# The scalars of a state-space recurrence: square roots moved from ScalarE's tables to VectorE, small steps packed in pairs, and all copies of the first FFT stage on ScalarE

## The chip, the cores and the metric

The kernel runs on one core of one Trainium2 chip. The metric is device time in microseconds (us) from launch to end; a number for a kernel is the median of several executions. Some executions are recorded by the hardware profiler. Its page and its trace give times counted from the start of the recorded span.

A core has five engines that each work through their own instruction queue in order: TensorE (PE in the profile, its weight loads PEld), VectorE (DVE), ScalarE (ACT), GpSimd (POOL) and SyncE (SP, which here only issues DMA transfers). They meet through semaphores[...].

## The reference, cut to what matters

Two branches work on the same `x` of 2048 positions by 1024 channels and are mixed by a gate per position.

```python
X = rfft2(x, axes=(-2, -1)); X = X * (w_r + 1j * w_i)
a = irfft2(X, s=(S, D)).astype(bfloat16)               # branch A

Lam = Lambda_re + 1j * Lambda_im                       # branch B, 1024 complex states
dt = exp(log_dt); Lam_bar = exp(dt * Lam)
B_bar = ((Lam_bar - 1.0) / Lam)[:, None] * (B_re + 1j * B_im)
h_t = Lam_bar * h_(t-1) + B_bar @ x_t                  # 2048 steps
b = 2 * Re(C @ h_t) + x * Dskip

g = sigmoid((x * gate_w).sum(-1)); out = g * a + (1 - g) * b
```

The change concerns how a few numbers per state are made from `Lambda_re`, `Lambda_im` and `log_dt` before branch B can start: the decay `r = exp(dt*Re Lam)`, the turn per step `thp` (in parts of a full turn), and the length `rho` and the angle of the complex factor `(Lam_bar - 1)/Lam`. The angle goes into a phase offset `beta`. The length needs a square root, the angle an arctangent.

## The kernel before, in words

**Branch A** is a 2-D FFT done with matrix products. In its first stage, `fstage(jj)` for jj = 0 to 7, two of sixteen slices of `x` (`xts[jj]`, loaded by `load_x`, 512 KB each, eight loads) are folded on VectorE into sums and differences: four instructions, L447 to L450, which write the tile `eo`. GpSimd mends the edge column with four tiny instructions, L452 to L455, in the order of the program. After every second slice, TensorE multiplies two `eo` tiles with the matrix `FW_sb` (L472 and L473), 8 products for each of four tiles `ps_f` in PSUM, and each `ps_f` is copied into the store `FX` (the same memory as `big`) by two copies of 128x512, L476 and L477. There are 16 such `ps_f` tiles and 32 copies; three `ps_f` can be alive at once. The names `eo` rotate over two buffers for even and two for odd jj, so `eo` of jj can be written only when TensorE has read `eo` of jj-4.

The second stage works in 16 groups: `fd(g)` (L488, copied out by L500), `bf_w(g)` (L511 to L520 into `ps_xe` and `ps_xo`, copied by L515 and L521, then multiplied with the filter by L525 to L528), and `bi(g)` (L546 to L549, copied by L550). The first `fd` reads all of `FX`.

**Branch B**: `ssm_pe` makes `B x` with TensorE (`psu`, L388) from the transposed `x` (`xT`) and the transposed B (`BT`); ScalarE scales it with `rho` or `nrho` (= -rho) on its way out (L390). `ssm_dve` turns by the phase tables `tab`, runs the scan with `r_sb` (L408) and turns back. The tables come from `tables(q)` (L357 to L368), which needs `thp` and `beta`.

**The scalars** sit at L278 to L344: small instructions on tiles of 128x8 numbers. ScalarE takes part with Exp (L279, L282), Sin (L304, L305), Sqrt (L323, L335), and a further Sin and Arctan (L339, L341).

**Loading**: SyncE issues the loads in the order of the program. The first transposed load, `load_BT(0)` (two of L211) with `load_xT(0)` behind it (two of L216), and all the B and filter loads behind those, do not start before the eight slices of `x` have landed: a copy of one column on GpSimd, L678 in the loop over `fstage`, writes into `BT` from the last slice and so holds them back. It stands in GpSimd's queue behind the edge columns of jj = 4 and ahead of those of jj = 5:

```python
for jj in range(8):
    for _ in fstage(jj):
        pass
    if jj == 4:
        nc.gpsimd.tensor_copy(out=BT[:, 0, 0, 0, 0:1], in_=xts[7][:, 0, 0:1])
        load_BT(0)
        load_xT(0)
```

**What sets the order**: in this part of the kernel GpSimd and SyncE keep the order in which the program is written. TensorE, VectorE and ScalarE do not: a scheduler of the framework orders their instructions by its own estimates when the program is built, so a change in one place can reorder them elsewhere. In the built program before, one product of `psu` stands in TensorE's queue ahead of ten of the sixteen first `fd` products.

Of the kernel before, what the change touches and what calls it, by code (L numbers as in the profile page):

```python
# [10 lines left out]
ACT = mybir.ActivationFunctionType  # L11
ALU = mybir.AluOpType
FP32 = mybir.dt.float32
BF16 = mybir.dt.bfloat16
I32 = mybir.dt.int32
# [7 lines left out]
P = 128  # L23
TC = 512
NCH = S // TC
MAGIC = 12582912.0
INV2PI = float(1.0 / (2.0 * np.pi))
TWO_PI_LO = 2.0 * float(np.nextafter(np.float32(np.pi), np.float32(0.0)))
# [108 lines left out]
def kernel(  # L137
# [17 lines left out]
    nc = tc.nc  # L155
    x = A_x[0]
# [23 lines left out]
    rp = ctx.enter_context(tc.tile_pool(name="rp", bufs=2))  # L180
# [77 lines left out]
    sp = cpool  # L258

    scr = rp.tile([P, 32, 8], FP32, name="scr", tag="su")  # L260
    scr_n = [0]

    def v8(name):
        if name in ("r_sb", "thp", "beta", "rho", "nrho"):
            return sp.tile([P, 8], FP32, name=name)
        scr_n[0] += 1
        return scr[:, scr_n[0] - 1, :]
# [7 lines left out]
    lre, lim, ldt = vec[:, 0, :], vec[:, 1, :], vec[:, 2, :]  # L275
    chpi = sp.tile([P, 1], FP32, name="chpi")
    nc.vector.memset(chpi, HALF_PI)
    dt = v8("dt")  # L278
    nc.scalar.activation(out=dt, in_=ldt, func=ACT.Exp)  # L279
    are = v8("are"); nc.vector.tensor_mul(out=are, in0=dt, in1=lre)  # L280
    r_sb = v8("r_sb")
    nc.scalar.activation(out=r_sb, in_=are, func=ACT.Exp)  # L282
    thp = v8("thp")
    nc.vector.scalar_tensor_tensor(out=thp, in0=lim, scalar=INV2PI, in1=dt, op0=ALU.mult, op1=ALU.mult)

    def frac(xx, n, nm, pool=sp, tag=None):
        kk = pool.tile([P, n], FP32, name=nm + "_k", **({"tag": tag} if tag else {}))
        nc.vector.tensor_scalar(out=kk, in0=xx, scalar1=MAGIC, scalar2=-MAGIC, op0=ALU.add, op1=ALU.add)
        nc.vector.tensor_sub(out=xx, in0=xx, in1=kk)
        nc.vector.tensor_scalar(out=kk.bitcast(I32), in0=xx.bitcast(I32), scalar1=0x7FFFFFFF, scalar2=None,  # L290
                                op0=ALU.bitwise_and)
        return xx, kk

    ang = sp.tile([P, 16], FP32, name="ang")
    nc.vector.tensor_copy(out=ang[:, 0:8], in_=thp)
    nc.vector.tensor_scalar_mul(out=ang[:, 8:16], in0=thp, scalar1=float(TC))
    rr, ra = frac(ang, 16, "ang")
    snc = sp.tile([P, 2, 16], FP32, name="snc")

    den = v8("den"); nc.vector.tensor_mul(out=den, in0=lre, in1=lre)  # L300
    den2 = v8("den2"); nc.vector.tensor_mul(out=den2, in0=lim, in1=lim)
    nc.vector.tensor_add(out=den, in0=den, in1=den2)
    inv = v8("inv"); nc.vector.reciprocal(out=inv, in_=den)
    nc.scalar.activation(out=snc[:, 0, :], in_=rr, func=ACT.Sin, scale=TWO_PI_LO)  # L304
    nc.scalar.activation(out=snc[:, 1, :], in_=ra, func=ACT.Sin, scale=-TWO_PI_LO, bias=chpi)  # L305
    sth, cth, sTC, cTC = snc[:, 0, 0:8], snc[:, 1, 0:8], snc[:, 0, 8:16], snc[:, 1, 8:16]
    sg = sp.tile([P, 8, 2], FP32, name="sg")
    nc.vector.tensor_scalar_mul(out=sg[:, :, 1], in0=sTC, scalar1=-1.0)
    nc.vector.tensor_copy(out=sg[:, :, 0], in_=sTC)
    lbi = v8("lbi"); nc.vector.tensor_mul(out=lbi, in0=r_sb, in1=sth)  # L310
    nr = v8("nr"); nc.vector.tensor_mul(out=nr, in0=r_sb, in1=cth)
    nc.vector.tensor_scalar_add(out=nr, in0=nr, scalar1=-1.0)
    t_a = v8("t_a"); nc.vector.tensor_mul(out=t_a, in0=nr, in1=lre)
    t_b = v8("t_b"); nc.vector.tensor_mul(out=t_b, in0=lbi, in1=lim)
    cr = v8("cr"); nc.vector.tensor_add(out=cr, in0=t_a, in1=t_b)
    t_c = v8("t_c"); nc.vector.tensor_mul(out=t_c, in0=lbi, in1=lre)
    t_d = v8("t_d"); nc.vector.tensor_mul(out=t_d, in0=nr, in1=lim)
    ci = v8("ci"); nc.vector.tensor_sub(out=ci, in0=t_c, in1=t_d)
    m2 = v8("m2"); nc.vector.tensor_mul(out=m2, in0=cr, in1=cr)
    m3 = v8("m3"); nc.vector.tensor_mul(out=m3, in0=ci, in1=ci)  # L320
    nc.vector.tensor_add(out=m2, in0=m2, in1=m3)
    mag = v8("mag")
    nc.scalar.activation(out=mag, in_=m2, func=ACT.Sqrt)  # L323
    rho = v8("rho")
    nc.vector.scalar_tensor_tensor(out=rho, in0=mag, scalar=2.0, in1=inv, op0=ALU.mult, op1=ALU.mult)
    nrho = v8("nrho")
    nc.vector.tensor_scalar_mul(out=nrho, in0=rho, scalar1=-1.0)
    hd = v8("hd"); nc.vector.tensor_add(out=hd, in0=mag, in1=cr)
    nc.vector.tensor_scalar_max(out=hd, in0=hd, scalar1=1e-30)
    nc.vector.reciprocal(out=hd, in_=hd)  # L330
    ht = v8("ht"); nc.vector.tensor_mul(out=ht, in0=ci, in1=hd)
    nc.vector.tensor_scalar(out=ht, in0=ht, scalar1=-1e15, scalar2=1e15, op0=ALU.max, op1=ALU.min)
    hq = v8("hq"); nc.vector.tensor_mul(out=hq, in0=ht, in1=ht)
    nc.vector.tensor_scalar_add(out=hq, in0=hq, scalar1=1.0)
    nc.scalar.activation(out=hq, in_=hq, func=ACT.Sqrt)  # L335
    nc.vector.tensor_scalar_add(out=hq, in0=hq, scalar1=1.0)
    nc.vector.reciprocal(out=hq, in_=hq)
    nc.vector.tensor_mul(out=ht, in0=ht, in1=hq)
    nc.scalar.activation(out=hd, in_=ht, func=ACT.Sin)  # L339
    fq = v8("fq")  # L340
    nc.scalar.activation(out=fq, in_=ht, func=ACT.Arctan)  # L341
    beta = v8("beta")
    nc.vector.tensor_scalar_mul(out=beta, in0=thp, scalar1=-255.5)
    nc.vector.scalar_tensor_tensor(out=beta, in0=fq, scalar=-2.0 * INV2PI, in1=beta, op0=ALU.mult, op1=ALU.add)  # L344

    tau_i = rp.tile([P, TC], I32, name="tau_i", tag="su")
    nc.gpsimd.iota(tau_i, pattern=[[1, TC]], base=0, channel_multiplier=0)
# [3 lines left out]
    def tables(q):  # L351
        xa = rp.tile([P, 2 * TC], FP32, name="xa", tag="cu")
        for jj in range(2):
            jb = 2 * q + jj
            xj = xa[:, TC * jj:TC * (jj + 1)]
            if q < 2:
                nc.vector.tensor_scalar(out=xj, in0=tau_f, scalar1=thp[:, jb:jb + 1], scalar2=beta[:, jb:jb + 1],  # L357
                                        op0=ALU.mult, op1=ALU.add)
            else:
                nc.scalar.activation(out=xj, in_=tau_f, func=ACT.Identity, scale=thp[:, jb:jb + 1],  # L360
                                     bias=beta[:, jb:jb + 1])
        rr, ra = frac(xa, 2 * TC, "xa", rp, "su")
        tq = tab[:, 2 * q:2 * q + 2]
        rr = rr.rearrange("p (a t) -> p a t", a=2)
        ra = ra.rearrange("p (a t) -> p a t", a=2)
        nc.scalar.activation(out=tq[:, :, 0, :], in_=ra, func=ACT.Sin, scale=-TWO_PI_LO, bias=chpi)
        nc.scalar.activation(out=tq[:, :, 1, :], in_=rr, func=ACT.Sin, scale=-TWO_PI_LO)
        nc.vector.tensor_scalar_mul(out=tq[:, :, 2, :], in0=tq[:, :, 1, :], scalar1=-1.0)  # L368
# [74 lines left out]
    def fstage(jj):  # L443
# [10 lines left out]
        nc.gpsimd.tensor_sub(out=eo[:, :, 1, 1, 0:1], in0=om, in1=eo[:, :, 1, 0, 0:1])  # L454
        nc.gpsimd.tensor_add(out=eo[:, :, 1, 0, 0:1], in0=om, in1=eo[:, :, 1, 0, 0:1])  # L455
        eos[jj] = eo
        if jj % 2 == 0:
            return
        j0 = 2 * jj - 2
        for eo_i in range(2):  # L460
            for b in range(2):
                ps = psF.tile([P, 4, 2, P], FP32, name="ps_f", tag="ps")
                bs = slice(P * b, P * (b + 1))
                for jl in range(4):
                    jt = jj - 1 + jl // 2
                    v = eos[jt][:, jl % 2, eo_i]
                    if jt in () and eo_i == 0:
                        los = [xts[jt][:, jl % 2, 512 * h + P * b:512 * h + P * (b + 1)] for h in range(2)]
                    else:
                        los = [v[:, 0, bs]]  # L470
                    for i, lo in enumerate(los):
                        nc.tensor.matmul(ps[:, jl], lhsT=lo, rhs=FW_sb[:, 0:2 * P], start=(i == 0), stop=False)  # L472
                    nc.tensor.matmul(ps[:, jl], lhsT=v[:, 1, bs], rhs=FW_sb[:, P * (1 + eo_i):P * (3 + eo_i)],  # L473
                                     start=False, stop=True)
                q = 4 * eo_i + 2 * b
                nc.scalar.copy(out=FX[:, q, :, j0:j0 + 4], in_=ps[:, :, 0, :].rearrange("p j c -> p c j"))  # L476
                (nc.vector.tensor_copy if (eo_i, b) in ((1,0),(1,1)) else nc.scalar.copy)(  # L477
                    out=FX[:, q + 1, :, j0:j0 + 4], in_=ps[:, :, 1, :].rearrange("p j c -> p c j"))
                yield 1.0

# [365 lines left out]
```

## Time and profile before

| what | value |
|---|---|
| median of 4 runs | 352.89 us (352.27 to 353.61) |
| the profiled execution's own time | 352.43 us |
| its span in the profile | 350.6 us |
| TensorE busy | 326.1 us, 93% of the span |
| VectorE busy | 297.6 us, 85% |
| ScalarE busy | 188.2 us, 54% |
| GpSimd busy | 42.2 us, 12% |
| last of the eight slices of `x` landed | 17.67 us (issued 9.94, landing 7.73 later) |
| first `psu` product | 29.27 us |

The profiled time is 1.83 us longer than its span. Busy shares are averages over stages with different limits; the stages of interest here are the first 40 us. In the trace's answers a line gives start, duration, engine, source line and operation, the tiles written and read, and in square brackets how long the engine stood idle before and what ended that. `SPq` and `ACTq` are issues of DMA transfers, which don't count as busy.

### The profile page before, as it was taken

The numbers are of one execution on the slowest core, as the hardware profiler recorded it, in microseconds if no ns is written. First come the engines' busy times: TensorE is split into PE (matmuls) and PEld (weight loads), VectorE is DVE, ScalarE is ACT, GpSimd is POOL, SyncE is SP. The second block draws the span as 40 slices with busy tenths as digits, with TensorE's granted clock in tenths as the row PEclk, the third lists the DMA queues.
The fourth block names the chain that finished last, engine by engine and source line by source line (L and its number), as shares of the span: only waits on it lengthen the run. The fifth ranks groups of instructions, "written<-read, shape, count | busy, mean of one in ns | idle before, by whom it ended". The sixth has DMA issues, their size and how long they took to land.

```text
span 350.6 us, 4890 instructions
## 1 busy us (share of the span) xinstructions
PE 326.1 (93%) x1804; PEld 173.6 (50%) x1804; DVE 297.6 (85%) x419; ACT 188.2 (54%) x255; POOL 42.2 (12%) x89
## 2 busy tenths in 40 slices
PE   2888999799979999999999999999989998999995
PEld 1675666466636566464444444444434443444442
DVE  3998859977999969898999999989798798988431
ACT  1997979679957877687253325241413404322240
POOL 4330422122110000000011000000000000000110
PEclk9999999989989999999999999999999999999999
DMA  7999999979796122113995054322413323444863
GB/s 270 349 140 213 221 230 212 185 157 198 179 225 111 63 98 81 62 60 125 226 235 166 12 167 119 92 90 62 150 41 110 92 60 109 103 134 135 265 194 112
DMA packets 68168, 51.30 MB, mean 146 GB/s; under 512 B 52656, under 2 KB 55728, under 8 KB 68144
## 3 DMA queue, kind: packets, MB, share of 16 engines
q1 hardware_dynamic: 64144, 38.75, 44.1%
q0 software_dynamic: 3648, 12.07, 14.1%
q8 instruction: 14, 0.23, 0.3%
q10 hardware_dynamic: 352, 0.17, 0.2%
q14 instruction: 10, 0.08, 0.1%
HBM read 21.61 MB, written 8.39 MB: 86 GB/s over the span
## 4 chain that ended last, share of the span: by engine, by line
PE 59%; DVE 20%; DMA 7%; ACT 7%; issue 4%; SPq 2%; POOL 0%; DVEq 0%; ACTq 0%; POOLq 0%
PE psy L782 26%; PE psu L388 20%; DVE su L408 7%; DMA xc<-in_A_x_dram 3%; PE ps_id L557 3%; PE ps_d L488 2%; ACT X L500 2%; DVE cu L403 2%; DVE cu L433 2%; DMA CT<-in_A_x_dram 2%; DMA xT<-in_A_x_dram 1%; PE ps_q L546 1%; DMA xt<-in_A_x_dram 1%; ACT u L390 1%; DVE t L526 1%
## 5 line engine op out<-in xcount | busy, mean ns | idle before, releaser
L388 PE MATMUL psu<-xT,BT 128*128 128x512 bf16 x512 | 121.2, 381 | 5.5 <-ACT u L390 4.2
L388 PEld LDWEIGHTS <-BT 128*128 128x128 bf16 x512 | 50.0, 98 | 61.7 <-issue 7.7
L408 DVE TENSOR_TENSOR_SCAN su<-r_sb,carry,cu 128x512 bf16<-128x512 f32 x48 | 57.7, 1265 | 0.4
L390 ACT ACTIVATE u<-psu,rho 128x512 bf16<-128x512 f32 x32 | 22.1, 690 | 65.2 <-PE psu L388 41.6
L767 POOL DMA_DIRECT2D xf<-gac x16 | 14.0, 873 | 216.7 <-ACT xf L766 216.7
L782 PEld LDWEIGHTS <-h 128*128 128x128 bf16 x256 | 25.1, 98 | 30.2
L390 ACT ACTIVATE u<-psu,nrho 128x512 bf16<-128x512 f32 x32 | 22.1, 691 | 29.3 <-PE psu L388 29.3
L764 ACT ACTIVATE gac<-gac,gf 128x1024 bf16<-128x1024 bf16 x16 | 18.3, 1141 | 28.1 <-DMA gac<-ya_scratch 28.1
L782 PE MATMUL psy<-CT,h 128*128 128x512 bf16 x128 | 28.9, 379 | 0.0
L782 PE MATMUL psy<-big,h 128*128 128x512 bf16 x128 | 28.9, 379 | 0.0
L760 DVE TENSOR_TENSOR xc<-xc,dsk_bc 128x1024 bf16<-128x1024 bf16 x16 | 11.0, 686 | 18.9 <-DMA xc<-in_A_x_dram 18.9
L789 DVE SCALAR_TENSOR_TENSOR o<-psy,om_f,xf 128x1024 bf16<-128x1024 f32 (+1 forms) x17 | 20.6, 1215 | 6.3 <-PE psy L782 6.3
L399 DVE TENSOR_TENSOR cu<-u,tab 128x2048 bf16<-128x2048 bf16 x16 | 19.5, 1220 | 5.4 <-ACT u L390 5.3
L550 ACT CAST big<-ps_q 128x1024 bf16<-128x1024 f32 x16 | 16.4, 1028 | 10.7 <-PE ps_q L549 10.5
L546 PE MATMUL ps_q<-MM,Y 128*128 128x256 bf16 x64 | 15.7, 280 | 4.7 <-DVE Y L527 4.6
L782 PEld LDWEIGHTS <-big 128*128 128x128 bf16 x128 | 12.5, 98 | 15.1
L782 PEld LDWEIGHTS <-xT 128*128 128x128 bf16 x128 | 12.5, 98 | 15.1
L403 DVE TENSOR_TENSOR cu<-cu,su 128x2048 bf16<-128x2048 bf16 x16 | 19.6, 1227 | 0.3
L433 DVE TENSOR_TENSOR cu<-su,tab 128x2048 bf16<-128x2048 bf16 x16 | 19.5, 1220 | 0.1
L488 PE MATMUL ps_d<-G_sb,big 128*128 128x256 bf16 (+3 forms) x128 | 19.6, 294 | 0.0
L435 DVE TENSOR_TENSOR u<-su,tab 128x2048 bf16<-128x2048 bf16 x16 | 19.5, 1218 | 0.0
L401 DVE TENSOR_TENSOR su<-u,tab 128x2048 bf16<-128x2048 bf16 x16 | 19.5, 1218 | 0.0
(168 smaller groups left out, 560.8 us busy)
## 6 DMA issues: line engine op xcount, KB each, us to landing
xf<-gac POOLq DMA_DIRECT2D x16, 512.0 KB, 4.1
ya_scratch<-ya SPq DMA_DIRECT2D x16, 256.0 KB, 2.0
xc<-in_A_x_dram SPq DMA_DIRECT2D x16, 256.0 KB, 3.2
gac<-ya_scratch SPq DMA_DIRECT2D x16, 256.0 KB, 3.3
out_dram<-o SPq DMA_DIRECT2D x15, 256.0 KB, 2.0
MM<-c_MM SPq DMA_DIRECT2D x16, 192.0 KB, 4.2
xt<-in_A_x_dram SPq DMA_DIRECT2D x4, 512.0 KB, 4.4
CT<-in_A_x_dram SPq DMA_DIRECT2D x4, 512.0 KB, 7.7
```

What stands on the lines that cost most here:

```text
L388: nc.tensor.matmul(psu, lhsT=BT[:, jb, ri, dblk, :], rhs=xT[:, dblk, TC * c:TC * (c + 1)], start=(dblk == 0), stop=(dblk == 7))
L390: nc.scalar.activation(out=u[:, jj, ri, :], in_=psu, func=ACT.Copy, scale=(nrho if ri else rho)[:, jb:jb + 1])
L399: nc.vector.tensor_mul(out=cu, in0=u, in1=tq[:, :, 0:1, :].to_broadcast(full))
L401: nc.vector.tensor_mul(out=su, in0=u[:, :, ::-1, :], in1=tq[:, :, 1:3, :])
L403: nc.vector.tensor_add(out=cu, in0=cu, in1=su)
L408: nc.vector.tensor_tensor_scan(out=su[:, jj, ri, :], data0=r_sb[:, jb:jb + 1].to_broadcast([P, TC]), data1=cu[:, jj, ri, :], initial=(0.0 ...
L433: nc.vector.tensor_mul(out=cu, in0=su, in1=tq[:, :, 0:1, ::-1].to_broadcast(full))
L435: nc.vector.tensor_mul(out=u, in0=su[:, :, ::-1, :], in1=tq[:, :, 1:3, ::-1])
L488: nc.tensor.matmul(ps[:, lo:lo + w], lhsT=FX[:, q, 8 * g:8 * g + 8, :], rhs=G_sb[:, o:o + w], start=start, stop=stop, skip_group_check=True)
L546: nc.tensor.matmul(dst, lhsT=Yr[:, e:e + 255:2], rhs=ri_, start=True, stop=False, **kw)
L782: nc.tensor.matmul(psy[:, ds], lhsT=hs[c, jb // 2][:, jb % 2, ri, P * tq:P * (tq + 1)], rhs=CT[dh][:, jb, ri, :], start=(i == 0), stop=(i ...
L789: nc.vector.scalar_tensor_tensor(out=o[:, ds], in0=psy[:, ds], scalar=om_f[:, tb:tb + 1], in1=xfs[tb][:, ds], op0=ALU.mult, op1=ALU.add)
```

## The change

The edits are these.

1. Both square roots become an inverse square root computed on VectorE (`rsqrt`): a first guess from the bits of the number and two Newton steps, seven dependent small instructions. The half-angle form of the arctangent is rewritten to need one such root, no square root of `1 + t*t`, and the Sin at L339 goes.
2. Real and imaginary parts are packed in pairs of 16 numbers where both get the same operation (`nl`, `pr`, `c2`).
3. Six small instructions go to GpSimd: two for |Lam|^2, `nrho`, the first half of `beta`, and the two of `sg`.
4. The scalars are a generator, `scalars()`. Its first piece is emitted before the first stage, and one further piece at the end of the folding of each `fstage(jj)`, jj = 0 to 5. This sets where its GpSimd instructions stand in GpSimd's queue: |Lam|^2 behind the edge columns of jj = 0, `nrho` behind those of jj = 3, `beta` and `sg` behind those of jj = 5.
5. All 32 copies of the first stage are made by ScalarE; before, eight of them (L477 for the second half of each set of four) were VectorE's.

```diff
-    dt = v8("dt")
-    nc.scalar.activation(out=dt, in_=ldt, func=ACT.Exp)
...
-    mag = v8("mag")
-    nc.scalar.activation(out=mag, in_=m2, func=ACT.Sqrt)
-    rho = v8("rho")
-    nc.vector.scalar_tensor_tensor(out=rho, in0=mag, scalar=2.0, in1=inv, op0=ALU.mult, op1=ALU.mult)
-    nrho = v8("nrho")
-    nc.vector.tensor_scalar_mul(out=nrho, in0=rho, scalar1=-1.0)
...
-    nc.scalar.activation(out=hq, in_=hq, func=ACT.Sqrt)
...
-    nc.scalar.activation(out=hd, in_=ht, func=ACT.Sin)
-    fq = v8("fq")
-    nc.scalar.activation(out=fq, in_=ht, func=ACT.Arctan)
...
+    def rsqrt(y, x, s):
+        nc.vector.tensor_scalar(out=y.bitcast(I32), in0=x.bitcast(I32), scalar1=-0.5, scalar2=float(0x5F3759DF),
+                                op0=ALU.mult, op1=ALU.add)
+        for _ in range(2):
+            nc.vector.tensor_mul(out=s, in0=y, in1=y)
+            nc.vector.scalar_tensor_tensor(out=s, in0=s, scalar=-0.5, in1=x, op0=ALU.mult, op1=ALU.mult)
+            nc.vector.scalar_tensor_tensor(out=y, in0=s, scalar=1.5, in1=y, op0=ALU.add, op1=ALU.mult)
+
+    def scalars():
+        dt, are = v8("dt"), v8("are")
+        nc.scalar.activation(out=dt, in_=ldt, func=ACT.Exp)
...
+        yield
+        dd, inv = v16(), v8("inv")
+        nc.gpsimd.tensor_mul(out=dd, in0=lam, in1=lam)
+        nc.gpsimd.tensor_add(out=dd[:, 0, :], in0=dd[:, 0, :], in1=dd[:, 1, :])
+        nc.vector.reciprocal(out=inv, in_=dd[:, 0, :])
+        yield
+        nl, pr, c2 = v16(), v16(), v16()
+        nc.vector.tensor_mul(out=nl, in0=snc[:, ::-1, 0:8], in1=r_sb.unsqueeze(1).to_broadcast([P, 2, 8]))
...
+        yield
+        m2, rs, mag, s = v8("m2"), v8("rs"), v8("mag"), v8("s")
+        nc.vector.tensor_mul(out=pr, in0=c2, in1=c2)
+        nc.vector.scalar_tensor_tensor(out=m2, in0=pr[:, 0, :], scalar=1e-30, in1=pr[:, 1, :], op0=ALU.add, op1=ALU.add)
+        rsqrt(rs, m2, s)
+        nc.vector.tensor_mul(out=mag, in0=m2, in1=rs)
+        yield
+        nc.vector.scalar_tensor_tensor(out=rho, in0=mag, scalar=2.0, in1=inv, op0=ALU.mult, op1=ALU.mult)
+        nc.gpsimd.tensor_scalar_mul(out=nrho, in0=rho, scalar1=-1.0)
...
+        yield
+        rsqrt(rs, m2, s)
...
+        yield
...
+        nc.scalar.activation(out=fq, in_=hd, func=ACT.Arctan)
+        nc.gpsimd.tensor_scalar_mul(out=beta, in0=thp, scalar1=-255.5)
+        nc.vector.scalar_tensor_tensor(out=beta, in0=fq, scalar=-2.0 * INV2PI, in1=beta, op0=ALU.mult, op1=ALU.add)
+        nc.gpsimd.tensor_scalar_mul(out=sg[:, :, 1], in0=sTC, scalar1=-1.0)
+        nc.gpsimd.tensor_copy(out=sg[:, :, 0], in_=sTC)
+        yield
+
+    chain = scalars()
+    for _ in range(1):
+        next(chain, None)
...
         eos[jj] = eo
+        for _ in range(1):
+            next(chain, None)
         if jj % 2 == 0:
             return
...
-                (nc.vector.tensor_copy if (eo_i, b) in ((1,0),(1,1)) else nc.scalar.copy)(
+                (nc.vector.tensor_copy if (jj, eo_i, b) in () else nc.scalar.copy)(
                     out=FX[:, q + 1, :, j0:j0 + 4], in_=ps[:, :, 1, :].rearrange("p j c -> p c j"))
```

The built program after the change has the same order on SyncE. On TensorE, VectorE and ScalarE the order differs in the first stage and in the first groups of the second, and is the same from there on. Three of the differences matter below: VectorE folds jj = 2 before it has finished jj = 1; `rho` stands on VectorE behind the first folding instruction of jj = 6; and TensorE has all sixteen of the first `fd` products ahead of `psu`, with seven `psu` products then in a row ahead of the first `ps_xe`.

More of the change, by code (lines that the diff above doesn't have):

```diff
@@ L277 @@
     nc.vector.memset(chpi, HALF_PI)
-    dt = v8("dt")
-    nc.scalar.activation(out=dt, in_=ldt, func=ACT.Exp)
[L280 to L287, printed above, removed]
+    r_sb, beta, rho, nrho = (v8(n) for n in ("r_sb", "beta", "rho", "nrho"))
@@ L288, in frac @@
+    ang = sp.tile([P, 16], FP32, name="ang")
+    angk = rp.tile([P, 2, 16], FP32, name="angk", tag="cu")
+    snc = sp.tile([P, 2, 16], FP32, name="snc")
+    thp = ang[:, 0:8]
+    sTC, cTC = snc[:, 0, 8:16], snc[:, 1, 8:16]
+    sg = sp.tile([P, 8, 2], FP32, name="sg")
+    lam = scr[:, 28:30, :]
+    def frac(xx, kk, ff):
         nc.vector.tensor_scalar(out=kk, in0=xx, scalar1=MAGIC, scalar2=-MAGIC, op0=ALU.add, op1=ALU.add)
-        nc.vector.tensor_sub(out=xx, in0=xx, in1=kk)
-        nc.vector.tensor_scalar(out=kk.bitcast(I32), in0=xx.bitcast(I32), scalar1=0x7FFFFFFF, scalar2=None,
+        nc.vector.tensor_sub(out=ff, in0=xx, in1=kk)
+        nc.vector.tensor_scalar(out=kk.bitcast(I32), in0=ff.bitcast(I32), scalar1=0x7FFFFFFF, scalar2=None,
@@ L291, in frac @@
                                 op0=ALU.bitwise_and)
[L292 to L321, printed above, removed]
-    mag = v8("mag")
-    nc.scalar.activation(out=mag, in_=m2, func=ACT.Sqrt)
-    rho = v8("rho")
-    nc.vector.scalar_tensor_tensor(out=rho, in0=mag, scalar=2.0, in1=inv, op0=ALU.mult, op1=ALU.mult)
-    nrho = v8("nrho")
-    nc.vector.tensor_scalar_mul(out=nrho, in0=rho, scalar1=-1.0)
@@ L328 @@
[L328 to L334, printed above, removed]
-    nc.scalar.activation(out=hq, in_=hq, func=ACT.Sqrt)
@@ L336, with v16 @@
-    nc.vector.tensor_scalar_add(out=hq, in0=hq, scalar1=1.0)
-    nc.vector.reciprocal(out=hq, in_=hq)
-    nc.vector.tensor_mul(out=ht, in0=ht, in1=hq)
-    nc.scalar.activation(out=hd, in_=ht, func=ACT.Sin)
-    fq = v8("fq")
-    nc.scalar.activation(out=fq, in_=ht, func=ACT.Arctan)
-    beta = v8("beta")
-    nc.vector.tensor_scalar_mul(out=beta, in0=thp, scalar1=-255.5)
-    nc.vector.scalar_tensor_tensor(out=beta, in0=fq, scalar=-2.0 * INV2PI, in1=beta, op0=ALU.mult, op1=ALU.add)
+    def v16():
+        scr_n[0] += 2
+        return scr[:, scr_n[0] - 2:scr_n[0], :]
@@ new lines, in rsqrt @@
+    def rsqrt(y, x, s):
[8 more added lines that the diff above has]
+        nc.scalar.activation(out=dt, in_=ldt, func=ACT.Exp)
+        nc.vector.scalar_tensor_tensor(out=thp, in0=lim, scalar=INV2PI, in1=dt, op0=ALU.mult, op1=ALU.mult)
+        nc.vector.tensor_scalar_mul(out=ang[:, 8:16], in0=thp, scalar1=float(TC))
+        frac(ang, angk[:, 0, :], angk[:, 1, :])
+        nc.scalar.activation(out=snc[:, 0, :], in_=angk[:, 1, :], func=ACT.Sin, scale=TWO_PI_LO)
+        nc.scalar.activation(out=snc[:, 1, :], in_=angk[:, 0, :], func=ACT.Sin, scale=-TWO_PI_LO, bias=chpi)
+        nc.vector.tensor_mul(out=are, in0=dt, in1=lre)
+        nc.scalar.activation(out=r_sb, in_=are, func=ACT.Exp)
+        yield
[6 more added lines that the diff above has]
+        nc.vector.tensor_mul(out=nl, in0=snc[:, ::-1, 0:8], in1=r_sb.unsqueeze(1).to_broadcast([P, 2, 8]))
+        nc.vector.tensor_scalar_add(out=nl[:, 0, :], in0=nl[:, 0, :], scalar1=-1.0)
+        nc.vector.tensor_mul(out=pr, in0=nl, in1=lam)
+        nc.vector.tensor_add(out=c2[:, 0, :], in0=pr[:, 0, :], in1=pr[:, 1, :])
+        nc.vector.tensor_mul(out=pr, in0=nl[:, ::-1, :], in1=lam)
+        nc.vector.tensor_sub(out=c2[:, 1, :], in0=pr[:, 0, :], in1=pr[:, 1, :])
+        yield
[7 more added lines that the diff above has]
+        nc.gpsimd.tensor_scalar_mul(out=nrho, in0=rho, scalar1=-1.0)
+        hd = v8("hd")
+        nc.vector.tensor_add(out=hd, in0=mag, in1=c2[:, 0, :])
+        nc.vector.tensor_scalar_max(out=hd, in0=hd, scalar1=1e-20)
+        nc.vector.tensor_mul(out=m2, in0=hd, in1=mag)
+        yield
+        rsqrt(rs, m2, s)
+        nc.vector.tensor_mul(out=m2, in0=m2, in1=rs)
+        nc.vector.scalar_tensor_tensor(out=hd, in0=m2, scalar=float(np.sqrt(2.0)), in1=hd, op0=ALU.mult, op1=ALU.add)
+        nc.vector.reciprocal(out=hd, in_=hd)
+        yield
+        nc.vector.tensor_mul(out=hd, in0=c2[:, 1, :], in1=hd)
+        nc.vector.tensor_scalar(out=hd, in0=hd, scalar1=-1.0, scalar2=1.0, op0=ALU.max, op1=ALU.min)
+        fq = v8("fq")
+        nc.scalar.activation(out=fq, in_=hd, func=ACT.Arctan)
[4 more added lines that the diff above has]
+        yield
@@ L361, in tables @@
                                      bias=beta[:, jb:jb + 1])
-        rr, ra = frac(xa, 2 * TC, "xa", rp, "su")
+        kk = rp.tile([P, 2 * TC], FP32, name="xa_k", tag="su")
+        frac(xa, kk, xa)
+        rr, ra = xa, kk
         tq = tab[:, 2 * q:2 * q + 2]
```

## The prediction

> **What bounds the kernel now.** I read the page's busy line first, then the chain that ended last around the first stage, then each engine's timeline there.
>
> ```profile
> PE 326.1 (93%) x1804; PEld 173.6 (50%) x1804; DVE 297.6 (85%) x419; ACT 188.2 (54%) x255; POOL 42.2 (12%) x89
> ```
>
> TensorE bounds the whole, so a change in the first 30 us counts by how it moves the point from which TensorE is kept busy. Beyond the first groups of the second stage the built orders agree on all engines, so I carry a shift there to the end one to one. The chain of waits, in order of time:
>
> ```profile
> 19.51 1.30 SPq L211
> 20.85 3.09 SPq L216
> 23.99 5.14 DMA xT<-in_A_x_dram
> 29.13 0.14 issue
> 29.27 0.38 PE psu L388
> ...
> 30.22 1.93 ACT X L500 x2
> 32.15 0.64 ACT X L515
> ```
>
> Not VectorE or ScalarE but the transposed load `xT` releases TensorE at 29.27, and what follows is ScalarE's work without a gap. What starts that load is in the timelines of GpSimd, SyncE and TensorE:
>
> ```profile
> 14.71 0.20 POOL L455 TENSOR_TENSOR eo<-om,eo 128x2 bf16<-128x2 f32 x1
> 17.72 0.37 POOL L678 COPY BT<-CT 128x1 bf16<-128x1 bf16 x1 [2.81 <-DMA CT<-in_A_x_dram]
> 18.05 0.20 POOL L452 TENSOR_TENSOR eo<-CT 128x2 bf16<-128x2 bf16 x1
> 18.12 1.34 SPq L211 DMA_TRANSPOSE BT<-in_B_B_re_dram  x1
> 29.27 0.38 PE L388 MATMUL psu<-xT,BT 128*128 128x512 bf16 x1 [1.25 <-DMA xT<-in_A_x_dram]
> ```
>
> GpSimd was idle 2.81 us when the last slice of `x` landed (17.67). From L678's start, 17.72, to `psu` is 11.55 us of issues and landing. VectorE and ScalarE, for prices:
>
> ```profile
> 12.50 0.17 DVE L312 TENSOR_SCALAR scr<-scr 128x8 f32<-128x8 f32 x1
> 12.70 0.17 DVE L313 TENSOR_TENSOR scr<-scr 128x8 f32<-128x8 f32 x1
> 12.79 0.16 DVE L317 TENSOR_TENSOR scr<-scr 128x8 f32<-128x8 f32 x1
> 13.62 1.28 ACT L323 ACT_TABLE_LOAD   x1
> 14.20 0.68 DVE L477 CAST big<-ps_f 128x512 bf16<-128x512 f32 x1
> 14.80 0.42 DVE L449 TENSOR_TENSOR eo<-CT 128x510 bf16<-128x510 bf16 x1
> 15.13 0.42 DVE L450 TENSOR_TENSOR eo<-CT 128x510 bf16<-128x510 bf16 x1
> ```
>
> A small instruction that needs the one before it follows after 0.20 (12.50 to 12.70); one that doesn't, after 0.08. A folding instruction takes 0.34 start to start, VectorE's copy of `ps_f` 0.60. ScalarE's copies start 0.48 apart (20.82, 21.30, 21.78 in its timeline).
>
> [...] The trace has the 1.28 (10.46, 13.62, 19.17)[...]: the next instruction follows at once. I use 1.3. [...] here a dependent one costs 0.12 more[...]. [...] four edge instructions take 0.97 from 18.05 to 19.02, and 1.47 beside the last folding, from 21.11 to 22.58. [...] Here products fall from 0.42 to 0.28 at 12.11, 3.6 us after TensorE resumed at 8.51.
>
> **The change, part by part.**
>
> ScalarE loses two table loads (sqrt, then back to sine; 2 x 1.3) and three activations (3 x 0.2), and gains eight copies (8 x 0.48 = 3.8): +0.6 us. VectorE loses eight copies (8 x 0.60 = 4.8 us) and keeps as many small instructions (39 before, 40 after; packing pays for the Newton steps). Taken alone this would end VectorE's part earlier. But TensorE does not wait for VectorE at 29.27, so I credit none of it.
>
> The start. VectorE folds jj = 2 ahead of jj = 1 and must wait for that slice, which lands at 8.02. The third folding of jj = 1, which the first tiles need, has four foldings and four small instructions ahead of it from there: 8.05 + 4 x 0.34 + 4 x 0.08 = 9.73 for its start rather than 8.07. Six products at the slow clock's 0.21 then move the first ScalarE copy from 9.36 to about 11.3. TensorE idles meanwhile and reaches the full clock near 12.8. From 14.3 ScalarE is steadily fed, at 0.96 per tile.
>
> When `rho` is ready. Ahead of it on VectorE from 8.05: 21 foldings at 0.337 = 7.1, 17 small ones at 0.08 = 1.4, four dependent Newton links at 0.20 = 0.8, so 17.3. In between, folding jj = 4 overwrites a tile that the fourth `ps_f` still reads; TensorE comes to it near 13.8 instead of 12.9, +0.9. So `rho` starts at about 18.2 and ends at 18.35.
>
> GpSimd's queue. `nrho` waits for that, and behind it stand the four edge instructions of jj = 4 and then L678. So 18.4, plus 0.2 to 0.4 for `nrho`, plus 0.97 to 1.47: L678 starts at 19.65 to 20.25, and I take 19.9. That is 2.2 us later than 17.72. The idle 2.81 us is used up, because `rho` is made after 17.67.
>
> What is late next. All four transposes are 2.2 us late: `xT` lands at 31.3, `psu` starts at 31.45. The edge columns also hold the tiles of jj = 4 and 5, ScalarE starves about 1.5 us near 19.2, and `FX` is complete at about 14.3 + 13 x 0.96 + 1.5 + 0.4 (last landing and Arctan) = 28.7, against 28.46 before. The first `fd` products end near 29.4, so TensorE idles until 31.45.
>
> Reordering gives some back. Before, `ps_xe` started at 31.29, 2.02 after `psu`, with ten `fd` products in between. Now only seven `psu` products stand between, 7 x 0.216 = 1.5: `ps_xe` at 32.96, +1.67. ScalarE's L515 (32.04 before) follows its last product: 32.96 + 0.33 + 0.27 + 0.04 = 33.6, +1.56. From there to L550 (38.28 before) ScalarE has seven instructions of the same kinds in either order, with no gap: the shift stays. Half a microsecond of cover is thin elsewhere: the filter matrices `MM` come through SyncE's queue, also 2 us late, and one of them landed at 51.71 for a product at 52.07. That allows 0.36, so the shift may grow to about 1.7. Gaps of the chain after that are releases between engines that all shift.
>
> Sum: span 350.6 + 1.65 = 352.25. The profiled execution took 1.83 more than its span: 354.1. The median of the runs was 0.46 above the profiled 352.43, so I predict 354.5 us for the median.
>
> Unknown rows. GpSimd on 128x8 and 128x16 tiles: not in the trace; between the 0.2 of its 128x2 rows and VectorE's 0.17 doubled, 0.35. Only `nrho` matters, and both ends are in the range of L678. A Newton step with integer bits on VectorE: like other 128x8 rows, 0.16 to 0.20. Bounds of L678: 18.7 if TensorE's cold start costs nothing, 20.8 if each row is at its dear end and the links cost 0.25. That is a shift from +0.4 to +2.6.
>
> **The rivals.**
>
> *Hidden, or a small gain.* If L678 starts by 18.2, the new order (1.5 between `psu` and `ps_xe` instead of 2.0) outweighs the delay. With no delay `ps_xe` starts at 29.27 + 1.51 = 30.8 and ScalarE comes to L515 at 31.4, a gain of 0.65 us and no more: 352.89 - 0.65 = 352.2 as a median. For it speaks the idle 2.81 us of GpSimd; against it, that 21 foldings alone need 7.1 us from 8.05. A delay of 1.0 would leave +0.4, 353.3: no change that can be told.
>
> *ScalarE becomes the bound.* With 32 copies and an Arctan in the midst that waits for the end of the chain on VectorE (near 22.7), `FX` would be late. For it: 16 tiles x 0.96 = 15.4 us, from 11.3. Against: the copies end at 28.7, and only from about 30.5 would they delay `ps_xe` more than `xT` does. If the chain is 2.5 us later than I think, this adds about 0.7: 355.2.
>
> *SyncE's queue lags on.* It issues almost without a gap from 18 to 52 us. If the full 2.2, or 2.8 with GpSimd slow, reaches `MM` in groups 5 and 6, the shift is 2.4: 355.3.
>
> *The clock.* Twice in the trace the granted clock is halved for 3.4 us after TensorE idled (70 to 74 and 101 to 104; 0.76 over 70 to 77). Another phase of the same waits can add or spare one of these, up to 1.7 us: 352.8 or 356.2.
>
> **How the numbers follow.** About 0.3% (1.06 us) is what a measurement of this kernel can tell from no change: 351.83 to 353.95. Forecast, a shift of 1.1 to 2.2: 0.45. ScalarE or SyncE beyond it: 0.18. Clock dearer: 0.05, cheaper 0.08. Hidden or a small rest: 0.17. Something that I don't see and that gains: 0.07. So slower 0.68 (forecast, the two beyond it, the dear clock), faster 0.12 (the unseen gain and a part of the cheap clock), same 0.20. For 8 in 10 the range goes from 352.0, the hidden case, to 356.4; the forecast's own is 353.9 to 355.0.
>
> **What would show it.** L678's row starts near 19.9, behind `nrho` and not behind a transfer. `psu`'s row waits for `xT` by 1.5 to 2.5 us, with `fd` products done before. ACT shows two table loads in the first 30 us and 32 copies 0.48 apart with a hole near 19. If L678 still starts at 17.7, or `psu` no longer waits for a transfer, the forecast is wrong at its root.

## The result and the profile after

The kernel after took 356.61 us in the median of 44 runs (352.16 to 360.95), the kernel before 353.47 us in 63 runs (350.04 to 358.5; the four known ones are among them). The ratio is 1.0049, with a 95% interval of 1.0029 to 1.0068: slower by half a per cent, 1.7 us on 353. Applied to the 352.89 us that were known, it is 354.6. Medians in this document are of all executions, while a ratio compares only those within 1.5% of the fastest of their kernel (26 of the 44 of after and, by the same rule, 53 of the 63 of before), so the two medians lie further apart, 3.1 us, than the ratio says. The profiled execution of after took 356.14 us and its span is 354.3 us.

All readings below give microseconds from the start of the span, in the columns that the prediction's lines have. First GpSimd's and SyncE's timelines of after, at the trigger of the transposed loads, and TensorE's at the first `psu`:

```profile
18.66 0.45 POOL L336 TENSOR_SCALAR nrho<-rho 128x8 f32<-128x8 f32 x1 [5.22 <-DVE scr L338]
...
20.38 0.19 POOL L697 COPY BT<-CT 128x1 bf16<-128x1 bf16 x1
20.60 1.33 SPq L211 DMA_TRANSPOSE BT<-in_B_B_re_dram  x1
30.62 1.67 PE L405 MATMUL psu<-xT,BT 128*128 128x512 bf16 x7 [1.00 <-DMA xT<-in_A_x_dram]
```

The trigger (L678 before, L697 now) no longer waits for a transfer. `nrho` waits 5.22 for VectorE, and nothing that stands behind it in GpSimd's queue starts before it: four edge instructions follow from 19.06 on, and then the trigger, at 20.38 instead of 17.72. But `psu` starts at 30.62, 10.24 after the trigger where before took 11.55, and TensorE waits for `xT` by 1.00 where it waited 1.25. Of the 1.31 less, 1.20 lie in the first transpose of `x`: from its issue to that of the second it took 3.14 before (20.85 to 23.99) and 1.94 after (23.95 to 25.89). The conversion L534 (L515 before) comes at 32.76 instead of 32.04 and L569 (L550 before) at 38.92 instead of 38.28. So at 39 us the whole delay is +0.6.

The time is lost five microseconds later. The waits of TensorE in the first 130 us of after (total, number, longest):

```profile
PE ps_xe L530 <- DMA MM<-c_MM: 3.4, 1, 3.4
...
PE psu L405 <- DMA xT<-in_A_x_dram: 1.0, 1, 1.0
```

The profile before has no wait on `MM` in that list. The chain that ended last, after:

```profile
23.95 1.89 SPq L216
25.89 2.19 SPq L216
...
36.58 2.26 SPq L211
38.89 2.45 SPq L211
41.44 5.20 DMA MM<-c_MM
46.69 0.28 PE ps_xe L530
```

It no longer runs through `xT` and ScalarE, as before, but through SyncE's row of issues to the load of one filter matrix, that of group 3. SyncE's timeline at this load, first before:

```profile
35.05 1.31 SPq L211 DMA_TRANSPOSE BT<-in_B_B_re_dram  x1
36.40 1.51 SPq L211 DMA_TRANSPOSE BT<-in_B_B_im_dram  x1
38.14 0.40 SPq L232 DMA_DIRECT2D MM<-c_MM  x1
```

and after:

```profile
36.58 2.26 SPq L211 DMA_TRANSPOSE BT<-in_B_B_re_dram  x1
38.89 2.45 SPq L211 DMA_TRANSPOSE BT<-in_B_B_im_dram  x1
41.44 0.54 SPq L232 DMA_DIRECT2D MM<-c_MM  x1
```

The two transposes ahead of the matrix took 2.82 to issue before and 4.71 after. TensorE's first product with this matrix, before and after:

```profile
42.52 0.27 PE L511 MATMUL ps_xe<-X,MM 128*128 128x256 bf16 x1
46.69 0.28 PE L530 MATMUL ps_xe<-X,MM 128*128 128x256 bf16 x1 [3.43 <-DMA MM<-c_MM]
```

The matrix landed at 41.81 before, 0.71 ahead of its product at 42.52. After, it landed at 46.64, for a product at 46.69. The 4.83 that it is later are 2.66 of later trigger, 0.64 more between trigger and issue (21.06 against 20.42), and 1.53 more from issue to landing (5.20 against 3.67).

From there the delay, taken as the same instruction of ScalarE in both traces, is +3.75 to 67 us, +2.44 from 73 to 244 us, 1.8 to 2.0 to 290 us and +3.7 at the end. The two large later steps are stretches of 3.41 us at half the clock of TensorE (granted clock 0.50 in all four, 1.00 just before). Each of the two traces has two of them there, one of them at different places: before from 70.1 and 100.9, after from 103.0 and 294.2.

### The profile page after: what moved, and what is told of

Read it like the earlier page. It is cut to its first block, busy times and chain, and to the rows that moved or that the text cites. A ratio compares the mean times of both kernels' runs of the same rounds, so it can differ in the third digit from the quotient of the medians.

```text
span 354.3 us, 4895 instructions
## 1 busy us (share of the span) xinstructions
PE 327.0 (92%) x1804; PEld 173.7 (49%) x1804; DVE 294.4 (83%) x412; ACT 188.7 (53%) x258; POOL 44.1 (12%) x95
## 4 chain that ended last, share of the span: by engine, by line
DVE 37%; PE 35%; DMA 9%; issue 6%; SPq 6%; ACT 5%; POOL 1%; DVEq 0%; ACTq 0%; POOLq 0%
PE psy L801 15%; DVE su L425 14%; PE psu L405 7%; DMA xc<-in_A_x_dram 4%; SPq L211 3%; DVE cu L420 3%; DVE cu L450 3%; PE ps_id L576 3%; DVE u L452 3%; DVE o L808 2%; DVE su L418 2%; DVE xc L779 2%; DVE cu L416 2%; DMA MM<-c_MM 1%; PE ps_d L507 1%
## 5 line engine op out<-in xcount | busy, mean ns | idle before, releaser
L569 ACT CAST big<-ps_q 128x1024 bf16<-128x1024 f32 x16 | 16.4, 1027 | 10.1 <-PE ps_q L568 9.8
L801 PEld LDWEIGHTS <-xT 128*128 128x128 bf16 x128 | 12.9, 101 | 16.2 <-issue 1.9
L507 PE MATMUL ps_d<-G_sb,big 128*128 128x256 bf16 (+3 forms) x128 | 18.7, 286 | 0.2 <-ACT big L496 0.2
```

Source lines behind the costliest of these rows:

```text
L507: nc.tensor.matmul(ps[:, lo:lo + w], lhsT=FX[:, q, 8 * g:8 * g + 8, :], rhs=G_sb[:, o:o + w], start=start, stop=stop, skip_group_check=True)
L801: nc.tensor.matmul(psy[:, ds], lhsT=hs[c, jb // 2][:, jb % 2, ri, P * tq:P * (tq + 1)], rhs=CT[dh][:, jb, ri, :], start=(i == 0), stop=(i ...
```

## The experiments

The theory at this point (**queue**): the later trigger costs little through `xT` and most through the filter matrix of group 3, which comes behind SyncE's transposes. Rivals: the delay of `xT` itself; the added ScalarE work; and, for any repair, that the DMA engines are short in this stretch whichever queue asks (**DMA**). The runs are in three groups, each with its own runs of before: medians 353.42 us (experiments 1 to 4), 354.49 (5 and 6) and 353.23 (7).

**1. `nrho` out of the trigger's way.** After, with one line moved:

```diff
-        nc.gpsimd.tensor_scalar_mul(out=nrho, in0=rho, scalar1=-1.0)
...
         nc.gpsimd.tensor_copy(out=sg[:, :, 0], in_=sTC)
+        nc.gpsimd.tensor_scalar_mul(out=nrho, in0=rho, scalar1=-1.0)
```

> The changed kernel with one move: nrho is made on GpSimd behind the sg pair (after the edge columns of jj = 5) and so no longer stands ahead of L697. Queue theory (the loss comes from L697 and with it SyncE's whole queue starting late, which reaches the filter matrix of group 3): L697 starts when the last slice of x lands, near 17.7 instead of 20.4; psu near 29.2 or earlier; the load of the filter matrix of group 3 is issued near 38.5 instead of 41.4; TensorE waits for that matrix 0.5 us or less instead of 3.4; time against the kernel before between -0.2% and +0.1%. Rival (the reordered front end on VectorE and TensorE and the copies on ScalarE cost the time): L697 moves all the same, but the time stays at +0.4 to +0.6%.

Ratio 1.0030 (1.0005 to 1.0056), 354.48 us. The trigger is at 18.42 and waits for `x` again, and up to group 2 the kernel is 0.3 to 0.5 us ahead of before. But the filter matrix is issued at 41.02 and lands at 45.65, and the wait of 3.4 us stays. SyncE's timeline:

```profile
35.92 2.22 SPq L211 DMA_TRANSPOSE BT<-in_B_B_re_dram  x1
38.19 2.73 SPq L211 DMA_TRANSPOSE BT<-in_B_B_im_dram  x1
41.02 0.53 SPq L232 DMA_DIRECT2D MM<-c_MM  x1
```

So a trigger 2 us earlier than in after does not cure the wait, and here the queue theory missed: SyncE took 22.6 us from the trigger to the matrix, not 20.4, and of these 2.2 us more, 2.1 lie in the two transposes just ahead of the matrix (4.95 against 2.82 before).

**2. The BT block behind the matrix.** After, with the fourth block of BT issued behind the matrix of group 3:

```diff
-        0: [lambda: load_BT(4)], 1: [lambda: load_BT(5)], ...
+        0: [lambda: load_BT(3), lambda: load_BT(4)], 1: [lambda: load_BT(5)], ...
...
-            load_BT(3)
```

> The changed kernel with one move on SyncE: load_BT(3) is issued behind the load of the filter matrix of group 3 instead of ahead of it; L697 stays late. Queue theory: L697 still starts near 20.4 and psu near 30.6, but the matrix is issued 3 to 4 us earlier, as soon as bi(0) has been through TensorE (near 38.7), and TensorE's wait for it goes; time against the kernel before 0 to +0.25%. A variant of the theory in which the late xT itself costs the time: +0.4% or more. Front-end rival: +0.4 to +0.6%.

Ratio 1.0079 (1.0050 to 1.0108), 356.47 us, where 0 to 0.25% was forecast. The wait left group 3 and came back in group 4, 3.3 us long: now four transposes stand ahead of that one. SyncE's timeline:

```profile
37.49 0.32 SPq L232 DMA_DIRECT2D MM<-c_MM  x1
37.86 1.23 SPq L211 DMA_TRANSPOSE BT<-in_B_B_re_dram  x1
39.14 3.38 SPq L211 DMA_TRANSPOSE BT<-in_B_B_im_dram  x1
42.56 2.17 SPq L211 DMA_TRANSPOSE BT<-in_B_B_re_dram  x1
44.77 1.75 SPq L211 DMA_TRANSPOSE BT<-in_B_B_im_dram  x1
46.62 0.52 SPq L232 DMA_DIRECT2D MM<-c_MM  x1
```

**3. The copies back.** After, with the eight copies on VectorE again:

```diff
-                (nc.vector.tensor_copy if (jj, eo_i, b) in () else nc.scalar.copy)(
+                (nc.vector.tensor_copy if (eo_i, b) in ((1,0),(1,1)) else nc.scalar.copy)(
```

> The changed kernel with the eight copies of the first stage given back to VectorE. Queue theory: the copies are not what costs; nrho still holds L697 to near 20 or later, since VectorE now has copies ahead of rho as well; the time stays at +0.4% or more. Rival (ScalarE's 32 copies cost the time): back to the kernel before, -0.1 to +0.15%.

Ratio 1.0162 (1.0108 to 1.0217), 359.32 us. With its eight copies kept, VectorE makes `rho` later: `nrho` at 20.65, the trigger at 22.65, and the first conversion +3.8 us. The queue theory's forecast (+0.4% or more) held, the rival's did not. So the new scalars without the move of the copies lose 1.6%; the move takes that down to the 0.5% of the whole.

**4. A late trigger alone.** Before, with a copy and five memsets on GpSimd in front of L678, which add no other work (they also hold back the edge columns that stand behind, as `nrho` does in after):

```diff
+            pad = cpool.tile([P, 512], BF16, name="pad")
+            nc.gpsimd.tensor_copy(out=pad[:, 0:1], in_=xts[7][:, 0, 0:1])
+            for _ in range(5):
+                nc.gpsimd.memset(pad, 0.0)
             nc.gpsimd.tensor_copy(out=BT[:, 0, 0, 0, 0:1], in_=xts[7][:, 0, 0:1])
```

> The kernel before with five memsets of 128x512 on GpSimd between the landing of the last slice of x and L678 (near 0.5 us each, so L678 near 20.4), and nothing else of the change. Queue theory: psu starts 1.3 to 2.7 us later than 29.27, the filter matrix of group 3 is issued near 41 and TensorE waits for it 2 to 4 us; time +0.5 to +1.0%. Front-end rival: the matrices are not what counts, 0 to +0.3%.

Ratio 1.0146 (1.0085 to 1.0207), 358.86 us, more than the +0.5 to +1.0% forecast. The five memsets took 2.85 together. The trigger starts 4.19 us later (21.91), 1.5 later than in after. Up to group 2 the delay is only 0.5 to 1.9 us. TensorE's waits:

```profile
PE ps_xe L511 <- DMA MM<-c_MM: 5.0, 2, 4.5
...
PE psu L388 <- DMA xT<-in_A_x_dram: 1.4, 1, 1.4
```

The matrix of group 3 is issued at 42.46, 4.32 later than before, and lands at 48.96, 7.15 later. The delay then jumps to +8.1. A late trigger in the kernel before, with none of the new scalars, makes the same wait on the same transfer.

**5. The copies alone.** Before, with all 32 copies on ScalarE and the old scalars:

```diff
-                (nc.vector.tensor_copy if (eo_i, b) in ((1,0),(1,1)) else nc.scalar.copy)(
+                (nc.vector.tensor_copy if (eo_i, b) in () else nc.scalar.copy)(
```

> The kernel before with the second half of the change alone: all copies of the first FFT stage on ScalarE, the old chain for the scalars with its three more activations and two more table loads kept. Theory of the start (ScalarE carries 8 copies of 0.75 us more and nothing leaves it): FX is complete 3 to 6 us later than the 28.7 us of before, the first conversion of group 0 shifts by +2 to +5 us, ratio 1.005 to 1.014. Rival (VectorE's freed time brings `rho` and so the copy ahead of the BT loads forward, and that pays for ScalarE's work): copy ahead of the BT loads before 17.0 us, ratio 0.996 to 1.002.

Ratio 0.9960 (0.9936 to 0.9985), 352.91 us: faster than before. The trigger is at 18.70 and the first conversion +1.7 us, so the late start that the first theory wanted is there. (Its 0.75 us for a copy was an estimate: ScalarE's busy time rises by 3.2 us for the eight, from 188.2 to 191.4.) But TensorE has no wait on `MM` in the list (the matrix lands at 44.04, ahead of its use), and the delay shrinks to 1.3 by 47 us. Both theories missed: the first the ratio, the second the place of the trigger. Why this kernel beats before is not known.

**6. The filter loads on GpSimd's queue**, from group 3 on, in after, in before, and in after with the late `nrho` of experiment 1:

```diff
-        nc.sync.dma_start(out=m, in_=cMM[g])
+        (nc.sync if g < 3 else nc.gpsimd).dma_start(out=m, in_=cMM[g])
```

> The kernel after, the loads of the filter matrices from group 3 on issued from GpSimd's queue instead of behind the BT transposes on SyncE's. Queue theory (the matrix of group 3 is late because SyncE is held by the transposes in front of it): it is issued near 38 us and lands near 42, PE's wait on MM falls from 3.4 us to under 0.7, the shift stays near +0.6 to +0.9 from 43 us on, ratio 0.994 to 1.000. Rival (the DMA engines themselves are behind, whichever queue asks): it lands after 45 us again or the next transfers in line (the W loads of GpSimd, the later matrices) come late by the same 3 us, ratio 1.003 to 1.007.

> The kernel before with the same move of the filter loads to GpSimd's queue. Queue theory: before has next to no wait on MM (group 3 landed 0.7 us ahead of its use), so nothing is won: ratio 0.998 to 1.002. Rival (the DMA engines are behind): transfers that share the engines with the W loads come late, ratio 1.002 to 1.006.

> The kernel after with both: `nrho` emitted behind `sg`, so that it does not stand ahead of the copy in front of the BT loads, and the filter loads on GpSimd's queue. Queue theory: trigger at 18.4, no wait on MM above 0.7 us, shift -0.5 to 0 throughout, ratio 0.990 to 0.997, below before and after. Rival (the DMA engines are behind): the matrix of group 3 lands after 45 us again, ratio 1.001 to 1.005 as with `nrho` late alone (1.0030).

Ratios 1.0136 (1.0070 to 1.0202), 1.0155 (1.0097 to 1.0214) and 1.0079 (1.0046 to 1.0113); medians 360.70, 360.58 and 360.41 us. All slower, the kernel before too. GpSimd's timeline of the second one (before, filter loads moved):

```profile
37.97 0.58 POOL L239 DMA_DIRECT2D W<-in_A_w_r_dram  x1 [1.75 <-DVE Y L525]
38.58 0.59 POOL L239 DMA_DIRECT2D W<-in_A_w_i_dram  x1
39.10 0.63 POOL L232 DMA_DIRECT2D MM<-c_MM  x1
```

The matrix is issued at 39.10 but lands at 46.29, 7.2 us later, and TensorE waits 9.3 us on `MM` in three places. The W load before it took 6.0 from issue to landing. So the queue theory was too simple, and GpSimd's queue no faster way: the matrix of group 3 took 3.7 (before) to 6.5 us (experiment 4) from issue to landing on SyncE's queue, and 6.4 to 7.5 on GpSimd's in the three kernels here. The move also reorders a few of TensorE's products, in after and in before, which these runs cannot separate.

**7. The matrix ahead of the crowd.** If neither queue delivers in time, the load has to be issued before the stretch: a fourth buffer, so that the matrix of group 3 goes out ahead of the BT transposes of blocks 2 and 3, and each later one a group earlier. No transfer is added or removed.

```diff
-        m = fr.tile([P, 6, P], BF16, name="MM", bufs=3)
+        m = fr.tile([P, 6, P], BF16, name="MM", bufs=4)
...
-            if g + 3 < 16:
-                load_M(g + 3)
+            if g + 4 < 16:
+                load_M(g + 4)
...
-            load_M(2)
+            load_M(2); load_M(3)
```

In after, in before, in before with the copies of experiment 5, and in after with the late `nrho` of experiment 1:

> The kernel after with a fourth buffer for the filter matrices: the one of group 3 is issued ahead of the BT transposes of blocks 2 and 3, every later one a group earlier. Queue theory (PE's wait on MM makes the loss): no wait on MM over 0.7 us, PE has no gap over 2 us between 40 and 50 us, the shift stays near +0.7, ratio 0.992 to 0.999, some 2 to 4 us under after; with the gap gone fewer half-clock stretches, so most executions at a granted clock of 0.99 or more. Rival (the DMA engines are short in this stretch, something else then comes late by as much: the W loads, the BT blocks): ratio 1.003 to 1.007 as after, with the gap of 2 to 4 us under another name.

> The kernel before with the same fourth buffer and order. If before itself loses to the wait on MM in executions other than the profiled one: ratio 0.994 to 0.998 and fewer executions under a clock of 0.99. If before never waits on MM: 0.999 to 1.002. DMA rival: above 1.002.

> The kernel before with all copies of the first FFT stage on ScalarE (0.9960 alone) and the fourth buffer. Its profile had no wait on MM left, so if the gain of the copies came from that wait: ratio 0.994 to 0.998, no better than alone. If the gain of the copies lies elsewhere and adds to that of the buffer: 0.990 to 0.994.

> The kernel after with `nrho` emitted behind `sg` (1.0030 alone) and the fourth buffer. Queue theory: without the wait of 3.4 us on MM the earlier trigger shows, shift -0.5 to 0 throughout, ratio 0.988 to 0.996, the fastest of all. DMA rival: 1.001 to 1.005.

| with the fourth buffer | median, us | ratio to before (95%) | without it |
|---|---|---|---|
| after | 352.12 | 0.9974 (0.9949 to 1.0000) | 1.0049 |
| before | 352.15 | 0.9977 (0.9952 to 1.0002) | 1 |
| before, copies on ScalarE | 352.65 | 0.9976 (0.9948 to 1.0005) | 0.9960 |
| after, `nrho` late | 351.66 | 0.9967 (0.9942 to 0.9991) | 1.0030 |

These runs decide. SyncE's timeline of after with the fourth buffer:

```profile
32.66 1.05 SPq L232 DMA_DIRECT2D MM<-c_MM  x2
...
36.88 3.46 SPq L211 DMA_TRANSPOSE BT<-in_B_B_re_dram  x1
40.38 2.59 SPq L211 DMA_TRANSPOSE BT<-in_B_B_im_dram  x1
43.06 0.53 SPq L232 DMA_DIRECT2D MM<-c_MM  x1
```

and TensorE's waits there:

```profile
PE psu L405 <- DMA xT<-in_A_x_dram: 1.0, 1, 1.0
...
PE ps_xe L530 <- DMA MM<-c_MM: 0.2, 1, 0.2
```

The transposes still take long (3.46 and 2.59), the trigger is still late (19.84), and `psu` still waits 1.0 for `xT`; all that has gone is the wait on the matrix. With it goes the whole loss, from 1.0049 to 0.9974, and after and before with the fourth buffer cannot be told apart (352.12 and 352.15). The two lead before by about a quarter of a per cent, with intervals that just reach no difference. After with the late `nrho` and the fourth buffer is faster than before and than after as they stand (0.9967, clear of 1); that is just short of the forecast of 0.988 to 0.996, and against the two plain four-buffer kernels its lead of 0.5 us is inside the intervals. The fourth buffer adds nothing to the copies alone, whose profile had no wait on `MM` to take away.

## Why the prediction was right, and where it was not

The direction and the size held: slower, 354.5 us forecast for 352.89, and the ratio makes it 354.6 (the medians of all executions, 3.1 us apart, would make it 356). The sum behind it did not hold, so that the number agrees so closely is luck. It put +1.65 us on the path through `xT`; that path carries about +0.6 at 39 us, and nothing that can be measured once the matrix is in time (experiment 7). The loss is a wait that the prediction named only as a rider and as one of its rivals.

**The copy behind `nrho`.** Right in its mechanism. `rho` starts at 18.41 (18.2 was forecast), `nrho` at 18.66, and L697 at 20.38 (19.9; the range given was 18.7 to 20.8). `nrho` took 0.40 to the next start and the edge instructions 1.32 from there to L697, the dear half of the 0.2 to 0.4 and the 0.97 to 1.47 that were allowed.

**The cold start.** The first ScalarE copy is at 10.93 (11.3), but the full clock comes at 14.1, not near 12.8, which was an estimate of the author's. With the same start of the program, products went from 0.42 to 0.27 near 12.4 in experiment 2, 12.9 in after with the fourth buffer, and 14.1 in after itself. What sets the point is not shown; over these 1.7 us a forecast to within a microsecond was not to be had. The fold of jj = 4 starts at 14.13, after a wait of 1.53 where +0.9 had been added for it; the folding had begun 0.35 earlier than assumed (7.70, not 8.05), so `rho` still came out near its forecast.

**ScalarE.** Right: two table loads of 1.28 each, 32 copies 0.48 apart, the last done at 29.05 (28.7). It was never the bound, as the rival *ScalarE becomes the bound* would have it; the copies alone, with all the old activations and loads, gave 0.9960.

**What is late next.** Here the term was mis-sized. "All four transposes are 2.2 us late: `xT` lands at 31.3" carried the 11.55 us from the trigger to `psu` over unchanged. It was 10.24, mostly because the first transpose of `x` held SyncE for less; why it did is open. The sign that `psu` would wait for `xT` by 1.5 to 2.5 us missed for the same reason: 1.00. `psu` came at 30.62 (31.45), `ps_xe` at 32.12 (32.96, +0.83 instead of +1.67), and L534 at 32.76 (33.6).

**"Half a microsecond of cover is thin elsewhere".** This step failed. It saw that the filter matrices come through SyncE's queue 2 us late, took the margin from one matrix that landed at 51.71 for a product at 52.07, and let the shift grow to 1.7 at most; the rival *SyncE's queue lags on* put the same at groups 5 and 6, for 0.75 us more. The runs showed group 3, where the margin before was 0.71, and a matrix that is 4.83 late, not 2.2: issue and landing stretch too. The wait was 3.43. What was missing was to follow each `MM` load's issue and landing through the queue, not the shift alone. Experiment 1 shows that an earlier trigger alone does not cure it, and experiment 4 that a late trigger is enough to cause it.

**The clock.** "Another phase of the same waits can add or spare one of these, up to 1.7 us" held, but a new wait adds chances for one. Leaving out the first 15 us and the last 6, the fourteen traces have 33 stretches at half clock, 31 of them 3.41 us long and two twice that, and 31 start within 1.5 us of the end of a gap of TensorE of 1.9 us or more. Of the 37 gaps of 2 us or more, 30 have one. A new wait on `MM` is such a gap. In after's own trace it drew none, but in experiment 1, where TensorE stood still from 42.3 to 45.7, the windows show it (the columns are stretch, its length, busy time of PE, PEld, DVE, ACT and POOL with their counts, the granted clock, the DMA share, GB/s):

```profile
44.00:46.00 2.00, 0.31 (x3) 0.29 (x4) 0.00 (x0) 0.00 (x0) 0.00 (x0) 1.00 1.11 322
46.00:48.00 2.00, 2.00 (x10) 1.10 (x9) 0.77 (x2) 0.73 (x1) 0.00 (x0) 0.56 1.20 272
```

Over all executions, the mean granted clock was under 0.987 in 29 of 149 of before, in 24 of 44 of after, and in none of 22 of after with the fourth buffer. Which of these executions waited on `MM` is not known, since only one of each kernel was profiled; that the gaps bring the lower clock fits and is not proved.

The traces also show what phase means here. In each of the fourteen, every change of the clock after the cold start lies a whole multiple of 3.413 us after the first full clock. Cut along this grid, they have some 1,370 periods. Each period in which TensorE stood idle for 1.97 us or more is followed by one at half clock; of the others, only one with 1.84 is (one with 1.91 is not), and two that were at half clock already, which makes the two double stretches. So in these traces a gap counts by its share of one period: in after (full clock from 14.26) the gap from 43.26 to 46.69 is cut at 44.98 into 1.72 and 1.71 and draws nothing; in experiment 1 (full clock from 12.10) 2.87 of the gap fall into one period, and half clock follows. Gaps well under one period draw it too: before has one of 2.30 us, ending at 69.50, with half clock from 70.14, and one of 2.26, ending at 99.98, with half clock from 100.86.

**One to one to the end.** Held: +2.44 from 73 to 244 us without a step, and after that only steps of the clock and of 0.6 us or less.

**From the profiled execution to the median.** The 0.46 us between the two came from four runs. Sixty-three runs give 353.47, 1.04 above the profiled 352.43. The profile before shows an execution without a wait on `MM`. With the fourth buffer the ratio of before is 0.9977, with an interval that reaches 1.0002, so a gain is not clear; that before loses to that wait in other executions would fit, and is not shown, since those were not profiled.

**What stays open.** What makes the transposes of B slow, and with them the way from trigger to matrix, 22.6 us in experiment 1 and 20.4 to 21.1 in before, after, and experiments 3, 4 and 5. The traces point to GpSimd's W loads (L239, the filter's factors for later groups), of which the first in this stretch is issued between 33.9 and 38.4 us. The fourth BT block's two transposes took 2.6 to 2.8 us together in the three traces where they are issued ahead of that load (before and the two with the old scalars and all copies on ScalarE), 3.4 and 3.7 where 0.4 to 0.5 us behind it, and 3.8 to 6.0 in the nine where 1.1 us or more behind. They are 0.1 ahead in before, 1.5 behind in after and 1.9 behind in experiment 1, whose W loads begin earlier too. That speaks for the place of the transposes against the W loads, more than the trigger alone. By what the one would slow the other is not shown. It is an order seen in the traces; no run moved the W loads or took them away.

## What to carry to other kernels

A change that delays the first of a row of transfers is to be priced at every transfer behind it, each with its own issue, landing and first use: the first consumer may wait no longer than before, and a later one pays. Look for the transfer with the least margin in the crowded stretch and issue it ahead of the crowd (a buffer more: 0.9974 for after here) rather than from another queue (1.0136). A new gap of TensorE is to be priced with the chance of a half-clock stretch on top: here 30 of the 37 gaps of 2 us or more had one of 3.41 us or twice that, and one of 3.41 costs up to 1.7, an estimate from half of its length.

## What had not been expected of the hardware

- An issue of a transpose of B on SyncE took 1.2 to 1.4 us in 139 of the 224 cases in the fourteen traces, and up to 4.43 us. Of the 49 over 2 us, 45 fell into a W load of GpSimd (from its issue to its landing), of the other 175, 108 did. All of it is SyncE's own time and holds up what stands behind.
- The filter load of 192 KB took 3.67, 5.20 and 7.2 us from issue to landing, in before, in after and from GpSimd's queue in experiment 6.
- Eight more copies on ScalarE, the engine on the chain of before, made the kernel faster (0.9960) although its profile shows the first conversion 1.7 us later. None of its 22 executions had a clock under 0.987, against 9 of 43 of before beside it.
- In the fourteen traces half-clock stretches of TensorE follow its gaps of 2 us or more in four of five cases (30 of 37), and last 3.41 us (31 of all 33) or twice that. They start on a grid of 3.413 us that begins with the first full clock, which came between 9.9 and 14.4 us; a gap of 3.43 us that the grid cuts in half drew none.
